# A fused attention, gated MLP and soft mixture-of-experts kernel: the first MLP block is cut in two halves around the second, and its weights are converted in pieces twice as wide

## The chip, the cores and the metric

The kernel runs on one NeuronCore of a Trainium2 chip. The metric is the device time of one execution in microseconds. Five engines work side by side, each through its own queue in order: PE (TensorE, matrix products; PEld loads its stationary operand), DVE (VectorE), ACT (ScalarE), POOL (GpSimd) and SP, which here issues nearly all DMAs.

## The reference, cut to what matters

```python
# 1. linear attention: 4 sequences, 8 heads, 576 positions, head 64, 128 features
def phi(x):
    proj = x @ w_phi
    proj = proj - max(abs(proj), axis=-1)
    return concat([exp(proj), exp(-proj)])
num = phi(q) @ (phi(k).T @ v);  den = phi(q) @ sum(phi(k)) + 1e-6
x = num / den                                  # 2304 tokens x 512
# 2. gated MLP, d_ff 1536
xn = x / sqrt(mean(x * x) + 1e-6) * rms_g
x = (silu(xn @ w_gate) * (xn @ w_val)) @ w_out
# 3. soft mixture of 8 experts, 4 slots each
logits = x @ phi;  d = softmax(logits, over tokens);  c = softmax(logits, over slots)
slot = d.T @ x;  slot_out[e] = relu(slot[e] @ w1[e]) @ w2[e]
return c @ slot_out
```

The MLP weights arrive as 64-bit floats, so the kernel turns them into 32-bit words itself.

## The kernel before, in words

The work falls into three stages. All large products are made of pairs of reduced-precision operands: a value is split into a high part (a cast) and a low part (value minus high part), and three products replace one.

**Key stage.** A loop over 18 tiles of 128 tokens (`TILES`) computes the key features and accumulates keys times values for each of the four sequences. Into its 36 half steps the queries of token block 0 are fitted (class `Turned`; the table `TURNED0` gives the half step of each part), and 16 of the 36 weight pieces are converted.

**MLP stage.** The tokens form 6 blocks of 384 (`BLK`). For each block the loop over `m` runs through 12 slices of 128 of d_ff: `gate` and `val` (12 matmuls each through `wide`, L826) and `out_tile` (9 matmuls, L851 to L853) which adds to three accumulators in PSUM. After each of the three comes a call of `fill()`, so a block has 36 slots; a table says what is done in which slot: the queries of the *next* block (`attend` is the product with keys and values for two heads, `scale` the root mean square, `out` the normalisation) and the softmax part `post` of the block *before* (`PSLOTS`). At the end of a block `split_block` makes the high and low parts of the next one's input `xraw` (ACT cast, DVE subtraction, both recorded as L100 and L103 of the helper `split`).

**Weights.** There are 3 x 6 weight tiles (`g`, `v`, `o` for each pair `j` of slices), each converted in two pieces of 128x512 (class `Conv`): a DMA, an ACT scaling (L125), three integer operations on DVE (L132 to L134), an ACT cast and a POOL subtraction into the weight tile. In block 0 one piece goes into each slot but every fifth, so all are done by slot 25; slice `m` of block 0 needs weight pair `m // 2`.

**Expert stage.** After the last block `finish` does its softmax part: it forms `xo` (the slot inputs), then the combine weights `c3`, turns them (`cturn`, L720) and stores them to memory (`cT_d`); two DMAs issued by ACT bring all combine weights back. Then come `fc1` (L960) and `fc2` (L976) of eight experts and the last product `combine` (L997), whose tiles go out on SP.

The order in each engine's queue is made by a scheduler when the program is built: it starts from the written order, and may put an operation that is ready in its model ahead of one that is not. It is fixed before the run. Buffer counts (`bufs`) limit it.

Of the kernel before, what the change touches and what calls it, by code (L numbers as in the profile page):

```python
# [26 lines left out]
NPRE = 16  # L27
# [3 lines left out]
CSKIP = 5  # L31
PSLOTS = [1, 4, 7, 12, 14, 16, 18, 20, 24]
REDUCED = [0, 0, 2, 3, 5, 6, 4, 8, 7, 11, 12, 9, 14, 12, 17, 18, 15, 20, 18, 23, 24, 27, 30]
TURNED0 = [2, 8, 14, 20, 12, 15, 20, 26, 28, 31]
TURNED1 = [0, 7, 14, 21, 6, 13, 20, 26, 28, 30]
# [26 lines left out]
def tile_kernel(ctx: ExitStack, tc: tile.TileContext, q2T, qT, kT, v, wbd, wg, wv, wo, rmsg, phi, w1, w2, consts, out):  # L62
# [44 lines left out]
    pieces = [(j, nm, c) for j in range(NJ) for nm in "gvo" for c in range(2)]  # L107
# [3 lines left out]
    class Conv:  # L111
# [3 lines left out]
        def __init__(self, sp, wp, key, bufs):  # L115
            self.sp, self.wp, self.key, self.bufs = sp, wp, key, bufs

        def load(self):
            j, nm, c = self.key
            self.raw = self.sp.tile([128, 512, 2], U32, tag="wraw", name="wraw", bufs=self.bufs[0])  # L120
            SP.dma_start(out=self.raw.rearrange("p n w -> p (n w)"), in_=wsrc[nm][j, :, 512 * c:512 * c + 512].bitcast(U32))

        def scale(self):
            self.w = self.wp.tile([128, 512], F32, tag="S", name="wt", bufs=self.bufs[1])
            ACT.activation(out=self.w, in_=self.raw[:, :, 1].bitcast(F32), func=AF.Copy, scale=2.0 ** -112)  # L125

        def join(self):

            w, hi, lo = self.w.bitcast(U32), self.raw[:, :, 1], self.raw[:, :, 0]
            shl, shr, band, bor = ALU.logical_shift_left, ALU.logical_shift_right, ALU.bitwise_and, ALU.bitwise_or  # L130
            return [
                lambda: DVE.tensor_scalar(out=w, in0=w, scalar1=3, scalar2=None, op0=shl),  # L132
                lambda: DVE.scalar_tensor_tensor(out=w, in0=hi, scalar=0x80000000, in1=w, op0=band, op1=bor),
                lambda: DVE.scalar_tensor_tensor(out=w, in0=lo, scalar=29, in1=w, op0=shr, op1=bor),  # L134
            ]

        def parts(self):
            j, nm, c = self.key
            if (nm, j) not in W:
                W[nm, j] = (wpA if j < 3 else wpool["B"]).tile([128, 2, 1024], F32R, tag="w", name=f"w{nm}{j}")  # L140
            u = W[nm, j]
            s = slice(512 * c, 512 * c + 512)
            split(u[:, 0, s], u[:, 1, s], self.w, hi_eng=ACT, lo_eng=POOL)

    conv_at = iter(pieces)
    convs = []

    scaled, joined = [], []

    def conv_load(sp, bufs, *pools):  # L150

        key = next(conv_at, None)
        if key is not None:
            n = pieces.index(key)
            c = Conv(sp, pools[n % len(pools)] if pools else sp, key, bufs)
            c.load()
            convs.append(c)
# [4 lines left out]

    def conv_scale():
        if convs:
            scaled.append(convs.pop(0))
            scaled[-1].scale()

    def conv_join(*between):
        ops = []
        if scaled:  # L170
            joined.append(scaled.pop(0))
            ops = joined[-1].join()
        for n in range(max(len(ops), len(between))):
            for f in between[n] if n < len(between) else ():
                f()
            if n < len(ops):
                ops[n]()
# [15 lines left out]
    class Q:  # L193
# [10 lines left out]
        def attend(self, c):  # L204
            if c == 0:
                xraw[self.blk] = xp.tile([128, 4, BLK], F32, tag="xraw", name="xraw", bufs=1)
# [56 lines left out]
    class Reduced(Q):  # L263
# [43 lines left out]
        def steps(self):  # L307
# [8 lines left out]
            return sorted(zip(REDUCED, s), key=lambda x: x[0])  # L316
# [71 lines left out]
    with ExitStack() as pk:  # L388
# [147 lines left out]
        for _ in range(3):  # L536
            conv_load(sp, (4, 3))
        conv_scale()
# [9 lines left out]
        qsteps = q0.steps(TURNED0[0:4], TURNED0[4:8], TURNED0[8:])  # L548
        qsteps = [[f for m, f in qsteps if m == n] for n in range(2 * TILES)]
        q0.begin()  # L550
        for i in range(TILES):
# [5 lines left out]
            if 0 < i < NPRE - 2:  # L557
                conv_load(sp, (4, 3))
# [11 lines left out]
            if kn:  # L570
                kn.project(0)
                kn.project(1)
                conv_join([lambda: kn.largest(0)], [lambda: kn.less(0), lambda: kn.largest(1)], [lambda: kn.less(1)])
# [61 lines left out]
    with ExitStack() as p2:  # L635
# [10 lines left out]
        def post(blk, x2):  # L646
# [12 lines left out]
            def logits():  # L659
# [7 lines left out]
                Mo, Mn = nM_run[(blk + 1) % 2], nM_run[blk % 2]  # L667
# [3 lines left out]
                DVE.tensor_scalar(out=Mn, in0=mx, scalar1=-1.0, scalar2=Mo if blk else None, op0=ALU.mult, op1=ALU.min if blk else ALU.bypass)  # L671
                if blk:
# [3 lines left out]
                ACT.activation(out=dT, in_=LT, func=AF.Exp, bias=Mn, accum_out=zb if blk else Z_run)  # L676
                if blk:
# [14 lines left out]
            def dispatch():  # L692
# [3 lines left out]
                if blk:  # L696
# [4 lines left out]
            def combine():  # L701
# [241 lines left out]
    with ExitStack() as p3:  # L943
# [60 lines left out]
        for e in range(NE):  # L1004
            fc1(e, 0)
# [79 lines left out]
```

## Time and profile before

| | |
|---|---|
| median of 3 runs | 763.22 us (761.87 to 764.25) |
| profiled execution | 764.22 us, its span 762.4 us |
| TensorE clock granted, mean | 0.98 of full speed |
| busy PE / DVE / ACT / POOL | 95% / 60% / 49% / 21% |
| key stage | 0 to 134.95 us |
| MLP block 0 | 134.95 to 244.95 us |
| MLP block 1 | 244.95 to 338.35 us |
| last accumulation of the MLP ends | 701.6 us |

The span runs from the first to the last instruction; 1.8 us of the time lie around it. The 40-slice view shows PE full from about 220 us to 700 us. Before that and after it there are gaps.

### The profile page before, as it was taken

What the parts mean: (1) busy time and instruction counts of PE and PEld (TensorE: products, weight loads), DVE (VectorE), ACT (ScalarE), POOL (GpSimd) and SP (SyncE); (2) the same over time, 40 slices, a digit from 0 to 9 for tenths busy, and PEclk for the clock granted to TensorE, in tenths of its full rate; (3) what the DMA queues carried; (4) which work ended last, traced back from release to release, by engine and by line L of the source; (5) the groups of instructions that cost most, each with busy time, mean ns of one, the idle gap of its engine ahead of it and who ended that gap; (6) DMA issues with size and microseconds to landing.
All of it is one profiled execution on the core that took longest, in us unless ns stands there. A gap on an engine that the chain in (4) does not pass through costs nothing.

```text
span 762.4 us, 12573 instructions
## 1 busy us (share of the span) xinstructions
PE 722.6 (95%) x4871; PEld 583.3 (77%) x4871; DVE 453.7 (60%) x875; ACT 373.3 (49%) x867; POOL 160.8 (21%) x128
## 2 busy tenths in 40 slices
PE   7997899986899999999999999999999999999895
PEld 4664555974788988899888989889888899988343
DVE  6898777899956556564564555645556453323213
ACT  6889675555744455435564345643465331212102
POOL 2663430446530211012110121101211010000000
PEclk9998999999999999999999999999999999999798
DMA  8762411554301110101000010000100046467698
GB/s 285 249 209 93 140 43 43 173 170 138 111 1 60 42 32 21 47 1 31 23 21 19 1 32 22 21 19 1 32 1 1 9 175 266 171 256 287 263 363 295
DMA packets 27739, 79.47 MB, mean 104 GB/s; under 512 B 2976, under 2 KB 13664, under 8 KB 23584
## 3 DMA queue, kind: packets, MB, share of 16 engines
q1 hardware_dynamic: 27456, 77.79, 29.7%
q10 hardware_dynamic: 224, 0.88, 0.4%
q8 instruction: 38, 0.62, 0.3%
q14 instruction: 21, 0.17, 0.1%
HBM read 71.99 MB, written 6.67 MB: 103 GB/s over the span
## 4 chain that ended last, share of the span: by engine, by line
PE 69%; ACT 1%; DVE 1%; issue 0%; ACTq 0%; DVEq 0%
PE pv L826 18%; PE pg L826 17%; PE acc L851 6%; PE acc L852 6%; PE acc L853 6%; PE num L213 3%; PE y L960 2%; PE y L976 2%; PE den L221 2%; PE x2tp L654 1%; PE qP L283 1%; PE qP L284 1%; PE op L997 1%; PE LT L664 1%; PE sps L695 1%; ACT qe L231 1%
## 5 line engine op out<-in xcount | busy, mean ns | idle before, releaser
L826 PE MATMUL pv<-xnh,wv 128*128 128x384 f32 x576 | 151.3, 343 | 1.0 <-DVE t L838 1.0
L826 PE MATMUL pg<-xnh,wg 128*128 128x384 f32 x576 | 150.0, 342 | 0.9 <-ACT xnh L100 0.5
L826 PEld LDWEIGHTS pg<-xnh,wg 128*128 128x128 f32 x576 | 104.9, 189 | 6.8 <-issue 0.9
L826 PEld LDWEIGHTS pv<-xnh,wv 128*128 128x128 f32 x576 | 102.8, 188 | 8.0 <-issue 6.7
L287 POOL PARTITION_ALL_REDUCE qe<-qe x32 | 50.0, 1563 | 247.1 <-ACT qe L286 227.4
L826 PE MATMUL pg<-xnl,wg 128*128 128x384 f32 x288 | 97.7, 339 | 0.0
L826 PE MATMUL pv<-xnl,wv 128*128 128x384 f32 x288 | 97.7, 339 | 0.0
L851 PE MATMUL acc<-wo,hh 128*128 128x512 f32 x216 | 88.0, 408 | 2.1 <-ACT hh L100 2.1
L852 PE MATMUL acc<-wo,hh 128*128 128x512 f32 x216 | 86.0, 398 | 0.0
L853 PE MATMUL acc<-wo,hl 128*128 128x512 f32 x216 | 85.5, 396 | 0.4 <-POOL hl L103 0.4
L100 ACT CAST hh<-t 128x384 fp32r<-128x384 f32 x72 | 36.7, 510 | 82.6 <-PE acc L852 67.7
L834 DVE SCALAR_TENSOR_TENSOR t<-t,pg 128x384 f32<-128x384 f32 x72 | 39.7, 551 | 52.5 <-ACT t L833 52.4
L833 ACT ACTIVATE t<-pg 128x384 f32<-128x384 f32 x72 | 35.1, 488 | 61.2 <-PE pg L826 61.2
L103 DVE TENSOR_TENSOR hl<-t,hh 128x384 fp32r<-128x384 f32 x62 | 34.5, 557 | 48.3 <-ACT hh L100 46.0
L231 ACT COPY qe<-qe 32x192 f32<-32x192 f32 x128 | 44.8, 350 | 31.7 <-DVE qe L226 30.4
L838 DVE TENSOR_TENSOR t<-t,pv 128x384 f32<-128x384 f32 x72 | 39.7, 551 | 28.9 <-PE pv L826 27.8
L826 PEld LDWEIGHTS pg<-xnl,wg 128*128 128x128 f32 x288 | 54.3, 188 | 0.3 <-DVE xnl L103 0.2
L826 PEld LDWEIGHTS pv<-xnl,wv 128*128 128x128 f32 x288 | 54.1, 188 | 0.1
L465 PE MATMUL kacc<-kp,vt 128*64 128x256 f32 (+1 forms) x320 | 43.5, 400 | 6.2 <-ACT kp L442 6.2
L853 PEld LDWEIGHTS acc<-wo,hl 128*128 128x128 f32 x216 | 40.7, 188 | 10.9 <-POOL hl L103 1.1
L851 PEld LDWEIGHTS acc<-wo,hh 128*128 128x128 f32 x216 | 40.9, 189 | 10.2 <-ACT hh L100 2.8
L852 PEld LDWEIGHTS acc<-wo,hh 128*128 128x128 f32 x216 | 40.8, 189 | 6.4
(202 smaller groups left out, 1241.0 us busy)
## 6 DMA issues: line engine op xcount, KB each, us to landing
eu<-in_w_dram SPq DMA_DIRECT2D x32, 1024.0 KB, 6.3
wraw<-in_wg_dram SPq DMA_DIRECT2D x12, 512.0 KB, 4.2
wraw<-in_wv_dram SPq DMA_DIRECT2D x12, 512.0 KB, 4.2
wraw<-in_wo_dram SPq DMA_DIRECT2D x12, 512.0 KB, 4.3
qraw<-in_qT_dram SPq DMA_DIRECT2D x32, 192.0 KB, 2.3
raw<-in_kT_dram SPq DMA_DIRECT2D x18, 256.0 KB, 4.0
vt<-in_v_dram SPq DMA_DIRECT2D x18, 256.0 KB, 3.9
out_dram<-ob SPq DMA_DIRECT2D x18, 256.0 KB, 3.1
```

What stands on the lines that cost most here:

```text
L100: ACT.copy(out=hi, in_=src)
L103: (lo_eng or POOL).tensor_tensor(out=lo, in0=src, in1=hi.bitcast(F32), op=ALU.subtract)
L231: ACT.copy(out=rd[64 * hh + 32 * r:64 * hh + 32 * r + 32, g], in_=dn[o:o + 32])
L287: POOL.partition_all_reduce(e[:, 0], e[:, 1], channels=128, reduce_op=bass_isa.ReduceOp.absmax)
L465: PE.matmul(out=kva[o0:o0 + 64, hh // 2], lhsT=self.vt[r0:r1, h], rhs=kp[r0:r1, hh].rearrange("p s f -> p (s f)"), start=first and hh < 2, ...
L826: PE.matmul(out=p, lhsT=w[:, a, c], rhs=x, start=n == 0, stop=n == 11)
L833: ACT.activation(out=t, in_=g, func=AF.Tanh, scale=0.5)
L834: DVE.scalar_tensor_tensor(out=t, in0=t, scalar=1.0, in1=g, op0=ALU.add, op1=ALU.mult)
L838: DVE.tensor_tensor(out=t, in0=t, in1=wide("v", m, xs), op=ALU.mult)
L851: PE.matmul(out=acc[i], lhsT=hh[:, s], rhs=w[:, 0], start=m == 0, stop=False)
L852: PE.matmul(out=acc[i], lhsT=hh[:, s], rhs=w[:, 1], start=False, stop=False)
L853: PE.matmul(out=acc[i], lhsT=hl[:, s], rhs=w[:, 0], start=False, stop=m == MF - 1)
```

## The change

- **Order of the MLP.** A list of phases replaces the loop over blocks: block 0 with slices 0 to 5 (18 slots), block 1 with all 12 (36 slots), block 0 with slices 6 to 11 (18 slots), then blocks 2 to 5. At the end of the first phase the three accumulators of block 0 are copied by ACT, halved, into a tile that a DMA writes to memory; it is read back before the third phase ends, and DVE adds it to the second half. `split_block` runs for block 0 twice. Its input `xraw` has a buffer of its own. The `post` of block 1 now comes first (in the third phase, table `PSHORT`), that of block 0 in the fourth.
- **Weights.** 18 pieces of 128x1024 replace 36 of 128x512. Six instead of eight tiles' worth are converted in the key stage, twelve in the MLP, at slots given by `CONVAT` over 40 slots. POOL makes the low part of the hidden values in the first 40 slots (`EARLY`); before, in block 0 until slice 9.
- **Queries.** Block 0's come some half steps earlier (`TURNED0`). The first half of block 1's (head pairs 0 and 1 and the first `attend`) moves into the key stage, the rest must be done by slot 14 instead of 30 (`TURNED1`). Block 2's queries begin at slot 24 of block 1 (`QSHIFT`).
- **Combine weights of the last block.** `cturn` and the two ACT DMAs come after four experts of `fc1` instead of before the first.

```diff
-NPRE = 16
+NPRE = 6
+KCONV, MCONV = 3, 2
-TURNED1 = [0, 7, 14, 21, 6, 13, 20, 26, 28, 30]
+TURNED1 = [-15, -8, 0, 5, -8, 0, 7, 11, 13, 14]
+PHASES = [(0, 0, MF // 2), (1, 0, MF), (0, MF // 2, MF)] + [(b, 0, MF) for b in range(2, NBLK)]
+CONVAT = [0, 3, 7, 12, 16, 19, 22, 25, 28, 31, 34, 37]
+QSHIFT, EARLY = 24, 40
...
-            self.raw = self.sp.tile([128, 512, 2], U32, tag="wraw", name="wraw", bufs=self.bufs[0])
+            self.raw = self.sp.tile([128, 1024, 2], U32, tag="wraw", name="wraw", bufs=self.bufs)
...
+        q1 = Turned(q1p, psk, 1, {"misc": 3, "raw": 1, "pr": 3, "e": 1})
+        q1steps = q1.steps(TURNED1[0:4], TURNED1[4:8], TURNED1[8:], lag=3)
+        q1.begin()
+        qsteps += [(m + 2 * TILES, f) for m, f in q1steps if m < 0]
+        q1steps = [(m, f) for m, f in q1steps if m >= 0]
...
+            if m1 < MF:
+                part = xp.tile([128, TPB, DM], F32, tag=XTAG[1], name="part", bufs=1)
+                for i in range(TPB):
+                    ACT.activation(out=part[:, i], in_=accs[p][i], func=AF.Copy, scale=0.5)
+                SP.dma_start(out=part_d, in_=part)
+                parts[blk] = None
+                return []
+            x2 = [x2_tile() for i in range(TPB)]
+            for i in range(TPB):
+                if blk in parts:
+                    DVE.scalar_tensor_tensor(out=x2[i], in0=accs[p][i], scalar=0.5, in1=parts[blk][:, i], op0=ALU.mult, op1=ALU.add)
+                else:
+                    ACT.activation(out=x2[i], in_=accs[p][i], func=AF.Copy, scale=0.5)
...
+        def fill():
+            n = slot[0]
+            slot[0] += 1
+            for at in CONVAT:
+                if n == at:
+                    conv_scale(piece_words)
+                if at <= n < at + 3:
+                    conv_join()
+                if n == at + 2:
+                    conv_load(sp, MCONV)
+                if n == at + 3:
+                    conv_parts()
+            for f in plan[n]:
+                f()
...
+            if after:
+                hs = split_h(t, slot[0] < EARLY)
...
         for e in range(NE):
+            if e == CTURN:
+                lastturn(ps.tile([96, TPB, 128], F32, tag="op", name="ctp", bufs=5), kl)
+                load_c()
             fc1(e, 0)
```

The queue of DVE at the end of block 1's queries, before. `den`, `e`, `xraw` and `s` belong to the last `attend`, `t` to the MLP, `ms` and `rs` to the root mean square:

```order
L225 TENSOR_SCALAR e_2630<-den 128x192
L226 RECIPROCAL e_2630<-e_2630 128x192
L232 TENSOR_TENSOR xraw<-xraw,e_2630 128x384
L834 SCALAR_TENSOR_TENSOR t<-t,pg 128x384
L239 TENSOR_TENSOR s<-s,e_2630 128x384
L838 TENSOR_TENSOR t<-t,pv 128x384
L250 TENSOR_SCALAR ms<-ssq 128x3
L186 TENSOR_SCALAR rs<-ms 128x3
```

The same place now (`wt` rows are weight conversion):

```order
L221 TENSOR_SCALAR e_2146<-den 128x192
L141 SCALAR_TENSOR_TENSOR wt<-wraw,wt 128x1024
L222 RECIPROCAL e_2146<-e_2146 128x192
L843 SCALAR_TENSOR_TENSOR t<-t,pg 128x384
L143 SCALAR_TENSOR_TENSOR wt<-wraw,wt 128x1024
L847 TENSOR_TENSOR t<-t,pv 128x384
L139 TENSOR_SCALAR wt<-wt 128x1024
L228 TENSOR_TENSOR xraw<-xraw,e_2146 128x384
L141 SCALAR_TENSOR_TENSOR wt<-wraw,wt 128x1024
L235 TENSOR_TENSOR s<-s,e_2146 128x384
L143 SCALAR_TENSOR_TENSOR wt<-wraw,wt 128x1024
L246 TENSOR_SCALAR ms<-ssq 128x3
```

Before, no weight conversion was left when the queue came to the last `attend`; now five conversion operations of two pieces stand between `den` and `ms`, the sixth and seventh of twelve pieces.

The queue of PE around the last product of block 1's normalisation (`r`), before, inside block 0's slice 11:

```order
L826 MATMUL pv<-xnh_1764,wv_2540 128x384 x2
L826 MATMUL pv<-xnl_1765,wv_2540 128x384
L826 MATMUL pv<-xnh_1768,wv_2540 128x384 x2
L365 MATMUL r<-dg,small 128x384
L826 MATMUL pv<-xnl_1769,wv_2540 128x384
L826 MATMUL pv<-xnh_1772,wv_2540 128x384 x2
```

The same product now, at the end of block 0's first half:

```order
L863 MATMUL acc_1861<-wo_2190,hl 128x512
L863 MATMUL acc_1862<-wo_2190,hl 128x512
L244 MATMUL ssq<-small,s 128x1 x3
L861 MATMUL acc_1863<-wo_2190,hh 128x512
L862 MATMUL acc_1863<-wo_2190,hh 128x512
L863 MATMUL acc_1863<-wo_2190,hl 128x512
L361 MATMUL r<-dg,small 128x384
L835 MATMUL pg<-xnh_2321,wg_284 128x384 x2
```

Before, seven matmuls of `val` and nine of `out_tile` stand between `r` and block 1's first `gate`; now three matmuls lie between `ssq` and `r`, and block 1's first `gate` stands right behind `r`.

The queue of PE at the start of the expert stage, before (`stp` gives the slot inputs, `ctp` turns the combine weights, `y` is `fc1`):

```order
L682 MATMUL L<-cst,l 128x96
L791 MATMUL stp<-G,S_run 128x32 x4
L720 MATMUL ctp<-cst,c_7124 96x128 x3
L960 MATMUL y_7145<-eu_6504,xo 32x512 x4
L960 MATMUL y_7145<-eu_6506,xo 32x512 x4
```

And now:

```order
L691 MATMUL L<-cst,l 128x96
L800 MATMUL stp<-G,S_run 128x32 x4
L1015 MATMUL y_6996<-eu_6362,xo 32x512 x4
L1015 MATMUL y_6996<-eu_6364,xo 32x512 x4
L1015 MATMUL y_6996<-eu_6366,xo 32x512 x4
L1015 MATMUL y_6996<-eu_6368,xo 32x512 x4
L729 MATMUL ctp<-cst,c_6982 96x128 x3
```

`ctp` has moved behind four experts of `fc1`.

## Rows read from the trace of the kernel before

**Rows 1.** Busy time of each engine by stretch (us), with granted clock, DMA share:

```profile
60.00:80.00 20.00, 16.04 (x138) 10.65 (x132) 15.81 (x30) 17.44 (x44) 6.17 (x7) 0.83 0.30 99
100.00:120.00 20.00, 19.43 (x186) 11.84 (x180) 14.46 (x25) 15.36 (x36) 7.38 (x8) 1.00 0.19 60
134.40:213.50 79.10, 67.14 (x401) 56.45 (x401) 71.96 (x107) 46.14 (x101) 41.82 (x30) 0.96 0.43 143
```

**Rows 2.** Timeline of PE: first gate of blocks 0, 1 and 2:

```profile
134.95 0.62 PE L826 MATMUL pg<-xnh,wg 128*128 128x384 f32 x2 [0.55 <-ACT xnh L100]
...
244.95 0.52 PE L826 MATMUL pg<-xnh,wg 128*128 128x384 f32 x2
...
338.35 0.52 PE L826 MATMUL pg<-xnh,wg 128*128 128x384 f32 x2
```

**Rows 3.** Waits of PE, 130 to 235 us (total, times, longest):

```profile
PE num L213 <- ACT e L357: 7.8, 4, 2.9
```

**Rows 4.** Timeline of PE: the ends of an out_tile and a projection, starts count:

```profile
144.16 0.39 PE L851 MATMUL acc<-wo,hh 128*128 128x512 f32 x1
...
146.27 0.28 PE L338 MATMUL P<-wbd_h,qxh 128*128 128x256 f32 x1
...
146.62 0.51 PE L826 MATMUL pg<-xnh,wg 128*128 128x384 f32 x2
```

**Rows 5.** The chain that ended last: one gate, one attend (start, us):

```profile
251.54 2.12 PE pg L826 x12
...
284.49 1.44 PE num L213 x8
285.93 0.79 PE den L221 x16
```

**Rows 6.** Groups of DVE by form, 134.4 to 215 us (busy us, mean ns):

```profile
L133 DVE SCALAR_TENSOR_TENSOR wt<-wraw,wt 128x512 uint32<-128x512 uint32 x20 | 22.0, 1098 | 0.4
L134 DVE SCALAR_TENSOR_TENSOR wt<-wraw,wt 128x512 uint32<-128x512 uint32 x20 | 20.7, 1037 | 0.2
L132 DVE TENSOR_SCALAR wt<-wt 128x512 uint32<-128x512 uint32 x20 | 12.0, 601 | 2.5 <-ACT wt L125 2.4
L838 DVE TENSOR_TENSOR t<-t,pv 128x384 f32<-128x384 f32 x8 | 4.3, 538 | 0.0
L226 DVE RECIPROCAL e<-e 128x192 f32<-128x192 f32 x3 | 4.0, 1344 | 0.0
L343 DVE TENSOR_REDUCE qmx<-P 128x2 f32<-128x256 f32 x9 | 3.7, 407 | 0.9 <-PE P L340 0.9
```

**Rows 7.** Timeline of DVE and POOL during weight conversion:

```profile
157.38 0.69 DVE L133 SCALAR_TENSOR_TENSOR wt<-wraw,wt 128x512 uint32<-128x512 uint32 x1
157.47 1.73 POOL L103 TENSOR_TENSOR wv<-wt,wv 128x512 fp32r<-128x512 f32 x1 [1.30 <-ACT wv L100]
158.11 1.64 DVE L134 SCALAR_TENSOR_TENSOR wt<-wraw,wt 128x512 uint32<-128x512 uint32 x1
```

**Rows 8.** Timeline from root mean square to block 1's first high part:

```profile
237.22 0.16 DVE L250 TENSOR_SCALAR ms<-ssq 128x3 f32<-128x3 f32 x1 [0.52 <-PE ssq L248]
...
241.82 0.61 DVE L261 SCALAR_TENSOR_TENSOR xraw<-xraw,small,r 128x384 f32<-128x384 f32 x1 [0.60 <-PE r L365]
...
242.46 1.09 ACT L100 CAST xnh<-xraw 128x384 fp32r<-128x384 f32 x2 [2.06 <-DVE xraw L261]
```

**Rows 9.** PE in the key stage: its longest wait, and that stretch:

```profile
71.78 3.68 PE L465 MATMUL kacc<-kp,vt 128*64 128x256 f32 x16 [3.88 <-ACT kp L442]
...
70.00:80.00 10.00, 8.22 (x56) 4.96 (x58) 7.77 (x15) 7.74 (x21) 2.77 (x3) 0.66 0.29 89
```

**Rows 10.** Expert stage: PE at its start, then stretches as in rows 1:

```profile
712.95 0.87 PE L720 MATMUL ctp<-cst,c 128*96 128x128 f32 x3 [2.09 <-DVE c L715]
...
720.00:745.00 25.00, 25.00 (x318) 11.16 (x310) 3.46 (x6) 1.49 (x6) 1.77 (x1) 1.00 1.01 362
745.00:750.00 5.00, 5.00 (x62) 2.95 (x62) 2.50 (x4) 1.75 (x4) 0.00 (x0) 1.00 0.74 254
```

More of the change, by code (lines that the diff above doesn't have):

```diff
@@ L106, in tile_kernel @@
     W = {}
-    pieces = [(j, nm, c) for j in range(NJ) for nm in "gvo" for c in range(2)]
+    pieces = [(j, nm) for j in range(NJ) for nm in "gvo"]
     wsrc = {"g": wg, "v": wv, "o": wo}
@@ L137, in parts @@
-        def parts(self):
[L138 to L143, printed above, removed]
+            if n == 1:
+                DVE.tensor_scalar(out=w, in0=w, scalar1=3, scalar2=None, op0=ALU.logical_shift_left)
+            elif n == 2:
+                DVE.scalar_tensor_tensor(out=w, in0=hi, scalar=0x80000000, in1=w, op0=ALU.bitwise_and, op1=ALU.bitwise_or)
+            else:
+                DVE.scalar_tensor_tensor(out=w, in0=lo, scalar=29, in1=w, op0=ALU.logical_shift_right, op1=ALU.bitwise_or)
@@ L145, in tile_kernel, with conv_load @@
+        def parts(self):
+            j, nm = self.key
+            u = W[nm, j] = (wpA if j < 3 else wpool["B"]).tile([128, 2, 1024], F32R, tag="w", name=f"w{nm}{j}")
+            split(u[:, 0], u[:, 1], self.w, hi_eng=ACT, lo_eng=POOL)
     conv_at = iter(pieces)
-    convs = []
-    scaled, joined = [], []
-    def conv_load(sp, bufs, *pools):
+    loaded, convs, joined = [], [], []
+    def conv_load(sp, bufs):
         key = next(conv_at, None)
         if key is not None:
-            n = pieces.index(key)
-            c = Conv(sp, pools[n % len(pools)] if pools else sp, key, bufs)
+            c = Conv(sp, key, bufs)
@@ new lines, in tile_kernel, with piece_words @@
+        q1.ps = ps
+        put(0, q1steps)
+        part_d = dp.tile([128, TPB, DM], F32, name="part_d")
+        wtile = wpB.tile([128, 2, 1024], F32, tag="w", name="wt")
+        words = []
+        for _ in range(2):
+            conv_load(sp, MCONV)
+        slot = [0]
+        def piece_words():
+            n = len(words)
+            words.append(n)
+            if n < len(CONVAT) - 1:
+                return wtile[:, n % 2]
+            return xp.tile([128, 1024], F32, tag=XTAG[1], name="wt", bufs=1)
@@ L933, in tile_kernel @@
         for i in range(TPB):
-            out_tile(MF - 1, hs, acc, i)
+            out_tile(p, MF - 1, hs, accs[p], i)
         mctx.close()
@@ L939, in tile_kernel @@
         unit(NX + 19)
-        post(NBLK - 1, [])(acc)
+        lastturn = post(NBLK - 1, [], NBLK - 1)(accs[p])
     with ExitStack() as p3:
```

272 lines of the change are left out of this document (135 added, 137 removed).

## The prediction

> **What bounds the kernel now.** I read the page's table of engines and its 40 slices first, to find where PE is not full; then the busy time by stretch, the timeline of PE at the block borders and its waits; then the queue of DVE where PE waits; last the expert stage.
>
> PE bounds the MLP stage from block 1 on: block 1 lasts 93.4 us, from 244.95 to 338.35 [rows 2], and the slices show PE full there. Block 0 lasts 110.0 us. Its own PE work is less than that. A slice has gate 2.12, val as much, out_tile 2.11 [rows 4, 5], so 6.35, and twelve make 76.2. Block 1's queries add twelve projections of 0.35 [rows 4], 4.2, four attends of 2.23 [rows 5], 8.9, and turns, `ssq` and `r`, some 4.2 by estimate (2.4, 0.9 and 0.9). That is 93.5, so block 0 loses 16.5 us. The waits named for PE there are for the exponentials ahead of `attend`, 7.8 us in four waits [rows 3], but what is late behind them is DVE: it is busy 71.96 of 79.1 us, 91%, while pieces are converted, against 67.14 for PE, at a granted clock of 0.96 [rows 1]. So DVE bounds block 0 for its first 79 us.
>
> The key stage, 135 us, is a mixture: PE is busy 19.43 of 20 us at 100 to 120, but 16.04 at 60 to 80, where it waits 3.88 us for ACT and then runs at a mean clock of 0.66 for ten us [rows 1, 9]. In the expert stage PE waits 2.09 us for the combine weights [rows 10]; from 720 to 745 the DMA engines are full, share 1.01.
>
> **The change part by part.**
>
> *A, key stage.* It takes on half of block 1's queries: six projections (2.1), one attend (2.2), six turns (1.2 by estimate), 5.5 us of PE, with their DVE and ACT work, in half steps 21 to 33, roughly 80 to 125 us. It loses four of its sixteen 512-wide conversions' worth, 2.74 us of DVE each (22.0, 20.7 and 12.0 us for 20 of them, [rows 6]), 10.9 us of DVE. If PE is full, the stage grows by 5.5. If the long wait of rows 9 does not form, because DVE and ACT are less crowded, it loses 3.9 of waiting and about 3.4 of slow clock (0.34 of 10 us): 5.5 less 7.3, about -2; with the small gaps of 80 to 100 also filled, -5. The bounds are -5 and +5.5. I take 0: PE fills its gaps of 60 to 100, the wait is partly there.
>
> *B, MLP up to the point where PE is full again.* The work of PE behind the key stage falls by the same 5.5. What counts is the time lost. The order of DVE shows that seven pieces stand ahead of `ms`, and that PE has nothing left at block 1's border but three matmuls between `ssq` and `r`. So block 1 cannot begin before DVE has gone through that queue. One 1024-wide piece: twice 2.74 less three fixed parts of about 0.1 (0.69 for 512 columns against 0.54 for 384 [rows 6, 7], so some 0.61 go with the columns), 5.2. Without a busy POOL beside it: two operations of 2 x 0.69 and one of about 0.9, 3.6. POOL is busy 41.82 of 79.1 us before [rows 1]; now it has in this stretch seven low parts of twice 1.4 and six of the hidden values at 1.2, 27 of some 65 us. So I take 4.7, nearer the row with POOL in it.
>
> The queue until `dg`: seven pieces 32.9; six slices of two operations at 0.54, 6.5; six projections of two operations at 0.41, 4.9; three attends of 0.36, 1.34 and two of 0.55, 8.4; the root mean square, eleven operations of 0.16 [rows 8] and one of 0.56, 2.3. Sum 55.0. In front lie 3.2 (gate, tanh and hand-over), behind it two more conversion operations, 2.8, while `r` runs, and 1.2 from the first normalisation to the first high part [rows 8]: 62.2 with DVE never idle, 67.6 with the 91% of rows 1. PE's own work there is 6 x 6.35, three attends, six projections, turns and `ssq`, `r`: 49.8. So 12.4 to 17.8 are lost, I take 15. After the border DVE has 4.3 pieces (20.2), splits and normalisation (4.6) and the slices' operations (4.4), 29.2, or 32 at 91%, while PE has 25.4 of matmuls to the fifth gate: 4 more, bounds 0 and 7. The loss is 19 against 16.5: with the 5.5 that moved, -3.0. With 3.6 a piece and no idle time it is 5 (then -17), with 5.2 and 91% it is 29 (then +7).
>
> [...] In rows 7 a DVE operation that takes 0.69 by itself takes 1.64, and ends 0.55 after the POOL operation does that began before it (159.20 and 159.75). [...]
>
> *C, what is added.* Three ACT copies of 128x512 lie beside gate and val; the write and the read of 786 KB have more than a block between them; block 0's second split is of an input long ready. POOL's low parts of hidden values now queue behind weight parts of 2.8 us instead of 1.4; out_tile has 4.2 us of gate and val ahead of it, so 0.5 + 2.8 + 1.2 is just too late at times. Post and queries of blocks 1 and 2 in 18 slots: PE has some 49 us there, DVE some 38. I take +0.5, bounds 0 and +3.
>
> *D, expert stage.* The wait of 2.09 us for the combine weights goes, and PE starts on `fc1` that much earlier; `ctp` itself stays. SP's queue now holds the write of the combine weights, which waits for four experts, in front of eight weight loads. ACT's read waits for that write, with its copy of `fc1`'s result behind it; both come about when they did. Past 745 us the stores decide: the DMA engines are full before and at 0.74 for 5 us [rows 10], so at most 1.3 us can be taken up there. I take -1.3, bounds -2.5 and +1.
>
> Sum: 0 - 3.0 + 0.5 - 1.3 = -3.8, from the profiled execution's 764.2 us (span 762.4 and 1.8 around it) 760.4. That execution is 1.0 above the median of the three runs, whose spread is 2.4; I say 760.0.
>
> **Rivals.**
>
> *R1, the queue of DVE decides (slower).* Place: the end of block 0's first half. Pieces cost 5.2 or more because POOL holds its operations of 2.8 us, so DVE reaches `ms` later, and the third attend's exponentials, behind ACT casts that themselves wait for DVE, come some 7 us late. The loss is 27 to 29, B +5 to +7; A and C at 0 and +1, D -1.3: 768 to 771. It decides from about 23 us lost in B. For it: the hoisted conversion in the order, 91% busy, rows 7. Against: the total of DVE's work in the MLP stage hardly grows, and block 1 has no post.
>
> *R2, both stalls go (much faster).* Conversion costs near 4 us a piece, the loss in B is about 12, so B is -10; A is -1. With C and D 752 to 753. For it: fewer, larger operations, and block 1's slices spread the rest. Against: the order has not spread the pieces over 40 slots as the table says, but put seven ahead of `ms`.
>
> *R3, nothing to measure.* The key stage is bound by PE where the queries go (19.43 of 20), A is +4, and takes back what B gives: 763 to 764.
>
> [...]
>
> **How the numbers follow.** The forecast has 0.40, own range 757 to 763; R1 0.25, R2 0.17, R3 0.18. What a measurement can tell from no change is about 0.3%, 2.3 us: faster is below 760.9, slower above 765.5. Of the forecast's share 0.28 lie below 760.9, of R2's all: faster 0.45. R1 gives slower 0.25 and R3's upper end 0.02, so 0.27; the rest, 0.28, is no change. The range runs from 752 (R2) to 769 (into R1); about 0.2 lie outside.
>
> **What would show it.** In the changed profile: A is right if the first gate starts at 133 to 137 us, and there is no wait of PE near 4 us at 60 to 80. B is right if block 1's first gate comes 62 to 68 us after block 0's, with DVE above 85% busy between them, and PE waits there for `ssq`, `r` and the first high part; L141 and L143 should take 1.7 to 1.9 us in the mean. C is right if the groups of acc show no waits above 1 us on POOL. D is right if `fc1` begins some 2.4 us after `stp` begins and stores end one us or so sooner relative to it. The forecast is wrong if block 1's gate comes later than 70 us (R1), earlier than 58 (R2), or the first gate after 139 (R3).

## The result and the profile after

The changed kernel takes 775.12 us (median of 769.06, 773.13, 777.10 and 782.47) against 762.84 before; the medians differ by 1.6%. The ratio, 1.0126 with a 95% interval of 1.0094 to 1.0158, leaves out the last of these times, since it lies over 1.5% above the fastest. The forecast was 760.0 and the range 752 to 769, so it was wrong in sign and in range. Two things have to be explained: the profiled execution, 769.06 us, is 4.8 longer than the one before, and the other executions of the same program are 4 to 13 longer still, where the kernel before repeats within 2.4.

In what follows, the border is the place where block 0's first half ends and block 1's first gate starts, and "gate to gate" is the time from block 0's first gate to that one. A held operation is one that is recorded as busy for longer than it takes by itself. All stretches are read from single profiled executions.

The timeline of PE after the change, in answer to [rows 2, 9, 10]: the key stage's wait, the first gates of blocks 0, 1 and 2, the last `out_tile`, and the start of `stp` and `fc1`.

```profile
73.75 2.00 PE L461 MATMUL kacc<-kp,vt 128*64 128x256 f32 x16 [1.44 <-DVE mx L420]
...
136.91 0.61 PE L835 MATMUL pg<-xnh,wg 128*128 128x384 f32 x2 [0.20 <-ACT xnh L107]
...
205.62 1.01 PE L835 MATMUL pg<-xnh,wg 128*128 128x384 f32 x2 [1.25 <-ACT xnh L107]
...
345.74 0.62 PE L835 MATMUL pg<-xnh,wg 128*128 128x384 f32 x2 [0.37 <-ACT xnh L107]
...
710.39 0.39 PE L863 MATMUL acc<-wo,hl 128*128 128x512 f32 x1
...
718.13 1.08 PE L800 MATMUL stp<-G,S_run 96*128 96x32 f32 x8 [0.19 <-DVE S_run L797]
719.64 0.64 PE L1015 MATMUL y<-eu,xo 128*32 128x512 f32 x4 [0.43 <-DVE xo L801]
```

The first gate and the last `out_tile` cut the profiled execution in three. The first gate is 2.0 us later than before (136.91 for 134.95). From it to the last `out_tile` it is 573.5 us for 566.3, 7.2 more (before, that instruction starts at 701.2). From there to the end of the span it is 56.9 for 61.2, 4.3 less. The sum is 4.9, the difference of the spans (767.3 and 762.4).

The busy time by stretch, columns as in [rows 1]; the third number from the end is the granted clock:

```profile
60.00:80.00 20.00, 18.38 (x180) 10.95 (x177) 16.21 (x26) 18.89 (x46) 8.81 (x9) 1.00 0.27 75
...
136.90:205.60 68.70, 55.50 (x330) 45.83 (x330) 58.34 (x79) 38.93 (x76) 27.67 (x14) 0.90 0.41 147
181.47:184.88 3.41, 3.41 (x28) 1.86 (x25) 1.17 (x3) 2.96 (x5) 1.46 (x2) 0.50 0.00 0
195.12:205.60 10.48, 5.40 (x13) 3.27 (x13) 8.72 (x19) 3.75 (x5) 2.67 (x2) 0.50 0.44 156
205.60:245.60 40.00, 36.00 (x169) 32.35 (x170) 30.16 (x31) 16.92 (x26) 21.42 (x10) 0.92 0.31 109
...
700.00:720.00 20.00, 17.96 (x111) 13.46 (x113) 8.74 (x30) 5.30 (x16) 0.95 (x1) 1.00 0.84 314
```

The waits of PE from block 0's first gate to block 1's (total, times, longest):

```profile
PE num L209 <- ACT e L353: 4.5, 1, 4.5
PE r L361 <- DVE dg L249: 3.5, 1, 3.5
PE acc L863 <- POOL hl L110: 2.5, 1, 2.5
PE pg L835 <- ACT xnh L107: 1.4, 2, 1.3
```

With 1.5 of smaller ones PE waits 13.4 us there; by the row of the whole stretch it is idle 13.2 of 68.7. The mean clock of 0.90 counts idle time as well. It comes from the two shorter rows: 13.9 us at a granted clock of 0.50. PE is busy in 8.8 of them and, by an estimate from the 0.50, loses half of that, 4.4 us. Without these 4.4 its 55.5 busy us are 51.1, and in a later run (e7) it is busy 51.12 over the same stretch at a clock of 1.00. So the 68.7 us are 51.1 of work, 13.2 of waiting and 4.4 of slow clock. Behind the border, to 346 us, PE is idle another 5.8 us, 3.8 of it `acc` waiting for `hl` and most of the rest for the splits of the blocks' inputs. Two more stretches at 0.50, with 6.6 us of work in them, add 3.3 by the same estimate.

Why DVE is late at the border is seen where its operations stand against POOL's. Groups of DVE by form from 137 to 240 us, in answer to [rows 6]:

```profile
L143 DVE SCALAR_TENSOR_TENSOR wt<-wraw,wt 128x1024 uint32<-128x1024 uint32 x12 | 22.0, 1830 | 0.1
L141 DVE SCALAR_TENSOR_TENSOR wt<-wraw,wt 128x1024 uint32<-128x1024 uint32 x12 | 18.3, 1525 | 0.2
L139 DVE TENSOR_SCALAR wt<-wt 128x1024 uint32<-128x1024 uint32 x12 | 10.5, 875 | 3.9 <-ACT wt L132 3.8
L235 DVE TENSOR_TENSOR s<-s,e 128x384 f32<-128x384 f32 x3 | 6.1, 2049 | 0.2 <-ACT e L234 0.2
...
L182 DVE TENSOR_SCALAR rs<-ms 128x3 uint32<-128x3 uint32 x1 | 2.0, 2050 | 0.0
```

A piece takes 4.23 us (the first three rows), less than the 4.7 of the prediction. But the sum of squares `s`, 0.555 us in the mean in the kernel before, takes 2.05 in the mean, and an operation on three columns 2.05, which took 0.17 before. The timeline of DVE and POOL shows what runs beside them:

```profile
176.12 3.17 POOL L110 TENSOR_TENSOR wg<-wt,wg 128x1024 fp32r<-128x1024 f32 x1 [3.59 <-ACT wg L107]
...
177.00 2.70 DVE L235 TENSOR_TENSOR s<-s,e 128x384 f32<-128x384 f32 x1
...
191.35 2.79 POOL L110 TENSOR_TENSOR wo<-wt,wo 128x1024 fp32r<-128x1024 f32 x1 [8.38 <-ACT wo L107]
...
192.14 2.42 DVE L235 TENSOR_TENSOR s<-s,e 128x384 f32<-128x384 f32 x1 [0.22 <-ACT e L234]
...
194.11 1.30 POOL L110 TENSOR_TENSOR hl<-t,hh 128x384 fp32r<-128x384 f32 x1
...
195.47 1.22 PE L863 MATMUL acc<-wo,hl 128*128 128x512 f32 x2 [2.53 <-POOL hl L110]
...
197.65 2.37 POOL L110 TENSOR_TENSOR wg<-wt,wg 128x1024 fp32r<-128x1024 f32 x1 [2.24 <-ACT wg L107]
...
198.00 2.05 DVE L182 TENSOR_SCALAR rs<-ms 128x3 uint32<-128x3 uint32 x1
```

Each of the three DVE operations begins while a low part runs on POOL and ends within 0.5 us of that part's end (179.70 and 179.29; 194.56 and 194.14; 200.05 and 200.02). The first and the third stand on the path: the exponentials for the next `num` write the buffer that the first `s` still reads, and `dg` follows the third operation. The second does not decide by itself. `ssq` needs it, but `ssq` stands on PE behind matmuls that wait until 195.47 for `hl`, and POOL begins `hl` only when the same low part is done. The two rows of `s`, which has two inputs, take 2.70 and 2.42 us for 0.555, and the third operation, with a single input, 2.05 for 0.17. By what means POOL holds them, no row shows.

### The profile page after: what moved, and what is told of

It reads as the page before. It is cut to its first block, busy times and chain, and to the rows that moved or that the text cites. A ratio compares the mean times of both kernels' runs of the same rounds, so it can differ in the third digit from the quotient of the medians.

```text
span 767.3 us, 12412 instructions
## 1 busy us (share of the span) xinstructions
PE 725.2 (95%) x4871; PEld 585.4 (76%) x4871; DVE 451.8 (59%) x824; ACT 369.4 (48%) x835; POOL 165.6 (22%) x114
## 4 chain that ended last, share of the span: by engine, by line
PE 73%; DVE 7%; DMA 7%; ACT 6%; issue 3%; POOL 3%; SPq 0%; POOLq 0%; ACTq 0%; DVEq 0%
PE pv L835 17%; PE pg L835 16%; PE acc L861 6%; PE acc L862 6%; PE acc L863 6%; PE num L209 4%; PE kacc L461 4%; DMA eu<-in_w_dram 3%; PE den L217 2%; PE kacc L470 2%; ACT e L227 2%; DVE wt L143 1%; DMA qraw<-in_q2T_dram 1%; DVE s L235 1%; DMA cT<-cT_d 1%
## 5 line engine op out<-in xcount | busy, mean ns | idle before, releaser
L110 DVE TENSOR_TENSOR hl<-t,hh 128x384 fp32r<-128x384 f32 x58 | 32.3, 557 | 45.9 <-ACT hh L107 45.9
L863 PEld LDWEIGHTS acc<-wo,hl 128*128 128x128 f32 x216 | 41.1, 191 | 17.8 <-POOL hl L110 8.0
```

Of the source, the lines that this page charges most:

```text
L110: (lo_eng or POOL).tensor_tensor(out=lo, in0=src, in1=hi.bitcast(F32), op=ALU.subtract)
L863: PE.matmul(out=acc[i], lhsT=hl[:, s], rhs=w[:, 0], start=False, stop=m == m1 - 1)
```

## Experiments

Each is an edit of the changed kernel, or of the kernel before where it says so; ratios are to runs of the kernel before on the same chip. Two theories recur. By Q, the length of DVE's queue ahead of the border decides. By L, POOL's low parts do, since they hold single operations of DVE and keep the hidden values waiting on POOL.

**e1, two pieces later.** The table's later slots are moved, and the later loads are made to wait for a value of block 1.

```
-CONVAT = [0, 3, 7, 12, 16, 19, 22, 25, 28, 31, 34, 37]
+CONVAT = [0, 3, 7, 18, 21, 24, 27, 30, 33, 36, 39, 42]
...
+            if after is not None:
+                ACT.copy(out=self.raw[:, 0].bitcast(F32), in_=after[:, 0:2])
...
-                    conv_load(sp, MCONV)
+                    conv_load(sp, MCONV, t if n >= 18 else None)
```

> Five pieces instead of seven are converted ahead of block 1's border: the loads of the later ones wait for a value of block 1 (by a copy of 128x2 on ACT into the tile that the load then fills). Theory Q (the length of DVE's queue ahead of the border decides): two pieces of 4.2 us leave the queue, block 1's first gate comes 60 to 62 us after block 0's (68.7 in the changed kernel), and the kernel is 5 to 8 us faster than the changed one. Theory L (single DVE operations are held while POOL has a low part of 2.7 us, and hidden values stand behind the low parts on POOL): the small operations at the border are still held by the pieces that stay, 66 to 69 us, and the time moves by less than 2 us.

Measured: 779.44 (768.31 to 783.90), ratio 1.0107 (1.0036 to 1.0177). Block 1's gate comes 61.6 us after block 0's (143.33 and 204.95), as theory Q had it, but nothing is gained. From the border to the last `out_tile` it is 8.6 us longer than in the changed kernel; the largest new wait there is one of 5.4 us at 293 us, for the exponentials of block 2's queries, which POOL prepares from 290 us on, behind the low part of a piece. The other loss is at the first gate, at 143.33 for 136.91, in a key stage that this edit does not touch. The same stretch of it in this kernel, and in the profile of the changed one:

```profile
104.00:118.00 14.00, 14.00 (x63) 6.64 (x64) 5.82 (x15) 4.47 (x11) 1.45 (x2) 0.51 0.07 19
```

```profile
104.00:118.00 14.00, 14.00 (x128) 8.46 (x127) 9.39 (x21) 8.41 (x20) 2.93 (x4) 1.00 0.14 40
```

PE is busy all the time in both, and gets through 63 instructions where it got through 128: the clock stands at 0.51 in the mean for 1.00. What it did before the fall, in e1:

```profile
101.13 0.36 PE L415 MATMUL P<-wbd_h,xh 128*128 128x256 f32 x1 [0.61 <-DVE pr L426]
...
101.68 0.73 PE L246 MATMUL ssq<-small,s 128*128 128x1 f32 x6
102.34 1.08 PE L463 MATMUL kacc<-kp,vt 64*64 64x256 f32 x8
103.35 0.64 PE L472 MATMUL kacc<-kp,small 64*32 64x256 f32 x8
```

A wait of 0.61 us, six matmuls of one column, and then those of the tile in which two sequences meet, with 64 rows instead of 128 (the half-height tile). The changed kernel's profiled execution has the same instructions and the same wait of 0.61 there, and no fall. In the kernel before, `ssq` stands at 118, amid whole projections.

**e2, low parts halved.**

```
-            split(u[:, 0], u[:, 1], self.w, hi_eng=ACT, lo_eng=POOL)
+            ACT.copy(out=u[:, 0], in_=self.w)
+            for s in (slice(0, 512), slice(512, 1024)):
+                POOL.tensor_tensor(out=u[:, 1, s], in0=self.w[:, s], in1=u[:, 0, s].bitcast(F32), op=ALU.subtract)
```

> The low part of a piece is made by two POOL operations of 128x512 instead of one of 128x1024; nothing else. Theory L: no DVE operation between 137 and 230 us is held by more than 1.5 us (now s 2.70 and 2.42 for 0.55, rs 2.05 for 0.16, wt 3.30 for 1.22), no wait of PE for hl is over 1.3 us (now 2.53 and 2.07), gate to gate 64 to 66 us, 3 to 5 us faster than the changed kernel. Theory Q: DVE has the same work in the same order, 68 to 70 us, within 1.5 us of the changed kernel.

Measured: 778.78 (772.05 to 780.86), ratio 1.0170 (1.0110 to 1.0229), gate to gate 66.1 us (145.21 to 211.30), with the fall in the key stage again (0.59 from 104 to 118, and the first gate 8.3 us later than in the changed kernel's profile). The timeline of DVE and POOL behind `ssq`:

```profile
203.40 2.51 POOL L150 TENSOR_TENSOR wg<-wt,wg 128x512 fp32r<-128x512 f32 x2
...
203.78 0.16 DVE L248 TENSOR_SCALAR ms<-ssq 128x3 f32<-128x3 f32 x1 [1.53 <-PE ssq L246]
203.97 0.73 DVE L184 TENSOR_SCALAR rs<-ms 128x3 uint32<-128x3 uint32 x1
...
204.74 1.19 DVE L185 TENSOR_SCALAR rs<-rs 128x3 uint32<-128x3 uint32 x1
```

At this place halving does not help: the hold is shorter, but the next small operation is held by the second half, 1.92 us for the two, where one took 2.05. Elsewhere it does. `s` takes 1.31 us in the mean for 2.05, the longest wait for `hl` is 1.9 us for 2.5 (1.3 was expected), and gate to gate is 2.6 us less, close to the 64 to 66 of theory L and below the 68 to 70 of theory Q. From the first gate to the last `out_tile` it is 571.0 us for 573.5. The 2.5 us do not show in the time, since the key stage loses more. So the remedy works in part, and a shorter hold is still a hold.

**e3, the late turns alone, on the kernel before.**

```
...
-                combine()
-                cturn()
+                combine(kl)
+                return cturn
...
         for e in range(NE):
+            if e == CTURN:
+                lastturn(ps.tile([96, TPB, 128], F32, tag="op", name="ctp", bufs=5), kl)
+                load_c()
             fc1(e, 0)
```

> The kernel before with one part of the change alone: the last block's combine weights are turned, written and read after four experts of fc1. If the gain of 4.3 us that the changed kernel shows behind the last block comes from this part (a wait of 2.1 us and the ten us at half clock that follow it), it is 3 to 5 us faster than before, and the granted clock stays at 1.00 from 700 to 740. If, as the prediction had it, the stores at the end take up all but 1.3 us, it is 0.5 to 2 us faster, and the slow clock is seen again or gone without a gain.

Measured: 759.72 (759.02 to 760.57), ratio 0.9939 (0.9918 to 0.9961): 4.1 us faster. The clock over 700 to 720 us is 1.00; before, it was 0.74. There it stood at 0.50 from 708.55 to 718.79, from 2.3 us ahead of the wait for the combine weights on, and PE was busy 8.0 of these 10.2 us, so by estimate half of that, 4.0, was lost. First the kernel before, then e3:

```profile
700.00:720.00 20.00, 16.79 (x103) 8.53 (x106) 8.03 (x31) 3.79 (x13) 0.98 (x2) 0.74 0.69 267
```

```profile
700.00:720.00 20.00, 18.37 (x153) 8.48 (x155) 8.73 (x32) 4.45 (x15) 2.76 (x2) 1.00 0.83 299
```

**e4, low parts on DVE.**

```
-            split(u[:, 0], u[:, 1], self.w, hi_eng=ACT, lo_eng=POOL)
+            split(u[:, 0], u[:, 1], self.w, hi_eng=ACT, lo_eng=POOL if j < 2 else DVE)
```

> The low parts of the twelve pieces in the MLP stage are made by DVE instead of POOL, which keeps the hidden values' alone. Theory L: DVE does 1.2 us more a piece, but its other operations are no longer held (4.2 us a piece now, of which 3.1 is what they take by themselves), so a piece with its low part takes 4.3 to 4.5; hidden values wait for nothing, gate to gate 62 to 66 us, 3 to 7 us faster than the changed kernel. Theory Q: seven pieces put 8 us more into the queue ahead of the border, 72 to 77 us, 4 to 8 us slower.

Measured: 768.12 (765.12 to 773.15), ratio 1.0061 (1.0035 to 1.0087). A piece with its low part takes 4.66 us on DVE, and without it, held by POOL, it took 4.23: POOL's hold had cost nearly as much as the work that POOL took over. The same three `s` as in the changed kernel now take:

```profile
L235 DVE TENSOR_TENSOR s<-s,e 128x384 f32<-128x384 f32 x3 | 2.1, 712 | 0.3 <-ACT e L234 0.3
```

That is 0.71 us in the mean for 2.05, and the operation on three columns takes 0.97 for 2.05. The waits for POOL behind the border are gone. At the border the queue is left: PE waits 2.95 for `s` and 5.95 for `dg`, since two pieces' operations now stand between `ms` and `dg`.

**e5, `ssq` moved in the key stage.**

```
-TURNED0 = [2, 7, 12, 17, 12, 14, 18, 23, 25, 27]
+TURNED0 = [2, 7, 12, 17, 12, 14, 18, 23, 29, 31]
```

> The changed kernel with block 0's scale and out issued later in the key stage (steps 29 and 31 instead of 25 and 27): on PE, ssq and r move behind block 0's last attend, away from the tile where two batches meet, whose matmuls have 64 rows. In two profiles of the variants so far, with the same key stage as the changed kernel, the granted clock stood at 0.50 from 104 to 118 us, in the profile of the changed kernel and in another it did not. Theory C (the short wait and the one-column matmuls of ssq just ahead of the half-height tile let the clock fall there in some executions, 6 to 7 us each time): no fall at 100 to 120, first gate at 136 to 138, the runs lie within 4 us of each other, median 767 to 771. Rival (the half-height tile does it by itself, or the fall comes anywhere): a fall in the key stage again, first gate at 139 to 146, runs spread over 8 us or more, median 773 to 779.

Measured: 771.75 (770.95 to 772.44), ratio 1.0102 (1.0077 to 1.0127), just above the 767 to 771 expected. The runs, 13 us apart in the changed kernel, lie within 1.5. The stretch that had half clock in e1:

```profile
104.00:118.00 14.00, 13.90 (x134) 8.46 (x136) 7.25 (x13) 10.69 (x26) 2.88 (x4) 1.00 0.14 34
```

The first gate is at 139.70, outside the 136 to 138 expected: the clock stood at 0.50 for 3.4 us each from 21 and from 76 us in this execution.

**e6 and e7, low parts on DVE and two pieces held back, and the same with `ssq` moved.** The edits of e4 and e1, with the table as it was and the condition below; e7 adds that of e5.

```
+                    conv_load(sp, MCONV, t if 14 <= n <= 18 else None)
```

> Low parts of the MLP stage's pieces on DVE as in the run before, and the loads of the sixth and seventh piece wait for a value of the fifth slice of block 0 and the first of block 1 (an ACT copy of 128x2 into the tile), so that five pieces stand ahead of block 1's ssq instead of seven, and none between ms and dg where two stood. If the queue of DVE at the border is what is left (waits of 2.95 for s and 5.95 for dg, then 16 us at half clock), block 1's first gate comes 56 to 61 us after block 0's (65.9), and it is 5 to 8 us faster than with the low parts alone, where no clock falls in the key stage 760 to 763. If the waits only move into block 1, as in the first run of later pieces, it is within 3 us of it.

> The same with ssq moved in the key stage as well. If both reasons hold and add up, the runs lie close together at 758 to 763, level with or below the kernel before; if the key stage's clock falls are not tied to ssq, 763 to 771 with a spread of 6 us or more.

Measured: e6 760.63 (753.90 to 765.24), ratio 0.9942 (0.9910 to 0.9973); e7 753.93 (751.79 to 756.54), ratio 0.9860 (0.9829 to 0.9891). e6's runs spread over 11 us, e7's over 5. e7 is below the 758 to 763 expected. In e6's profile, the slowest of its ten executions, the key stage has its fall (0.59 from 104 to 118, first gate 146.08), in e7's it has not. The border in e7, and the stretch ahead of it:

```profile
138.62 0.62 PE L837 MATMUL pg<-xnh,wg 128*128 128x384 f32 x2 [0.20 <-ACT xnh L107]
...
187.97 0.80 PE L246 MATMUL ssq<-small,s 128*128 128x1 f32 x6 [1.78 <-DVE s L237]
...
191.88 0.88 PE L363 MATMUL r<-dg,small 128*128 128x384 f32 x2 [0.90 <-DVE dg L251]
...
194.02 0.62 PE L837 MATMUL pg<-xnh,wg 128*128 128x384 f32 x2 [1.25 <-ACT xnh L107]
```

```profile
138.60:194.00 55.40, 51.12 (x330) 43.71 (x330) 46.49 (x76) 34.36 (x72) 9.39 (x7) 1.00 0.36 125
```

Gate to gate is 55.4 us for 68.7, at a granted clock of 1.00.

**e8, the kernel before with late turns and low parts on DVE.** Added to e3's edit:

```
-            split(u[:, 0, s], u[:, 1, s], self.w, hi_eng=ACT, lo_eng=POOL)
+            split(u[:, 0, s], u[:, 1, s], self.w, hi_eng=ACT, lo_eng=POOL if pieces.index(self.key) < NPRE else DVE)
```

> The kernel before with the late turns and with the low parts of the MLP stage's 20 pieces of 128x512 on DVE. If POOL's low parts hold DVE there as well (the three operations of a piece take 2.74 us in the mean, by themselves about 1.7, with the low part 2.4), DVE has some 6 us less to do in block 0, block 0 takes 103 to 107 us instead of 110 and the kernel 753 to 757 us. If the holds cost nothing there because each of POOL's operations is short, DVE has more to do and block 0 takes 110 to 114 us, the kernel 759 to 763.

Measured: 750.72 (750.29 to 753.40), ratio 0.9835 (0.9806 to 0.9863), 9.0 below e3 and below the 753 to 757 expected. The stretch of the last row of [rows 1]:

```profile
134.40:213.50 79.10, 75.32 (x467) 66.96 (x468) 74.60 (x131) 50.78 (x114) 13.94 (x12) 0.98 0.43 142
```

PE is busy 75.32 us for 67.14. DVE is no less busy, 74.60 for 71.96: its three operations and the low part take 2.87 us a piece, where the three alone took 2.74.

**e9 and e10, each of e7's two edits alone, on e5.**

```
-            split(u[:, 0], u[:, 1], self.w, hi_eng=ACT, lo_eng=POOL)
+            split(u[:, 0], u[:, 1], self.w, hi_eng=ACT, lo_eng=POOL if j < 2 else DVE)
```

```
+            if after is not None:
+                ACT.copy(out=self.raw[:, 0].bitcast(F32), in_=after[:, 0:2])
...
-                    conv_load(sp, MCONV)
+                    conv_load(sp, MCONV, t if 14 <= n <= 18 else None)
```

> The kernel with ssq moved (771.75 us, runs within 1.5 us), and the low parts of the MLP stage's pieces on DVE: one of the two edits of the 753.9 us kernel alone. Two pieces still stand between ms and dg. If POOL's low parts cost mainly behind the border (hidden values queued behind them, DVE held), 5 to 7 us go, 764 to 767, gate to gate 65 to 67 (69.4), no wait for POOL. If DVE's queue is all there is to it, more DVE work gains nothing: 770 to 776.

> The kernel with ssq moved, and only the loads of the sixth and seventh piece made to wait, low parts on POOL: the other edit alone. If the queue ahead of the border is a cause by itself, gate to gate 58 to 62 us, 762 to 766. If the holds by POOL keep the border late or the pieces left out come back as waits in block 1, 766 to 771; with the edits adding up, the sum of both gains is 17 to 18 us.

Measured: e9 761.82 (759.44 to 765.31), ratio 0.9978 (0.9956 to 1.0000), gate to gate 65.8 us; e10 768.34 (764.62 to 770.60), ratio 1.0052 (1.0032 to 1.0072), 61.8 us. From 771.75 the low parts alone gain 9.9, the pieces held back alone 3.4, both together 17.8, which is 4.5 more than the sum. Ahead of the border the queue is the larger part: gate to gate falls from 69.4 us by 3.6 in e9, by 7.6 in e10 and by 14.0 with both (e7). But with low parts on POOL the pieces held back return behind the border as waits for hidden values: 5.9 of the 6.2 us in the first row stand there, while the wait in the second row is ahead of it (e10, from 138 to 300 us):

```profile
PE acc L865 <- POOL hl L110: 6.2, 5, 2.6
PE num L211 <- ACT e L355: 4.5, 1, 4.5
```

**e11, hidden values' low parts on DVE, on e5.**

```
-QSHIFT, EARLY = 24, 40
+QSHIFT, EARLY = 24, 0
```

> The kernel with ssq moved, and the low parts of the hidden values of the MLP stage on DVE from the first slices on, those of the pieces on POOL: it tells the queue on POOL (hidden values behind low parts of 2.7 us) from the hold of DVE. If the queue on POOL is what the move of the low parts gains, the waits for hl (6.3 us) and the slow clock behind them go, 765 to 768. If the hold of DVE is, DVE gets 0.56 us more a slice and is held as before, gate to gate 70 to 74 us, 771 to 777.

Measured: 774.60 (774.02 to 776.26), ratio 1.0141 (1.0125 to 1.0157), gate to gate 75.3 us. The waits for POOL go (6.3 us), and the kernel is 2.9 slower: what leaves POOL's queue goes to a DVE that has more to do, and PE waits 5.5 us for `dg`, 3.5 in e5. So e11 shows that this is no remedy, but not what the queue on POOL costs by itself; e9 takes away both the hold and the queue and gains 9.9.

**e12, fewer pieces in the key stage, on e8.**

```
-NPRE = 16
+NPRE = 12
```

> The kernel before with late turns and low parts on DVE (750.7 us), with 12 instead of 16 pieces of 128x512 converted in the key stage, as many columns as in the changed kernel. If the key stage's wait of 3.9 us and the half clock behind it come from the conversion work there, the wait falls under 2 us and the first gate comes at 129 to 132 instead of 134.2; the MLP stage takes four pieces of 2.9 us more on a DVE that is 96% busy, 8 to 12 us for PE less what its own work covers. Sum: 750 to 756 if DVE decides, 745 to 748 if the wait was the dearer.

Measured: 747.79 (747.61 to 749.81), ratio 0.9793 (0.9777 to 0.9809), the fastest kernel here. In the timeline of PE, its longest wait between 60 and 80 us and the first gate, and then that stretch as in [rows 1]:

```profile
68.81 0.36 PE L418 MATMUL P<-wbd_h,xh 128*128 128x256 f32 x1 [1.39 <-ACT kp L442]
...
128.35 0.62 PE L827 MATMUL pg<-xnh,wg 128*128 128x384 f32 x2 [0.55 <-ACT xnh L101]
```

```profile
60.00:80.00 20.00, 18.43 (x177) 12.14 (x178) 17.68 (x34) 19.28 (x49) 7.33 (x10) 1.00 0.21 65
```

The wait and the half clock of [rows 9] are gone, and the first gate comes 5.9 us earlier than in e8 (134.24). The time falls by 2.9 us. In the profiled executions the stretch from the first gate to the last `out_tile` gives back 4.7 (560.9 us for 556.2), and the expert stage is 2.2 shorter.

## Why the prediction was wrong

Of the 15.1 us between the forecast and the median, 8.7 show in the profiled execution (A 2.0, B and C 9.7, D -3.0, counted from 760.4). The rest is the spread between executions, of which the clock in the key stage explains a part.

**A, the key stage (0, bounds -5 and +5.5).** In the profiled execution it was +2.0, and the wait of [rows 9] fell to 1.44 us, as said. Fewer pieces are worth 5.9 (e12; 7.3 was written, with 3.4 for a slow clock that counted idle time too: PE is busy 5.3 of the 6.8 us at 0.50 there, which is 2.7). The queries, 5.5 by estimate, cost up to the 8.6 between the first gates of e12 and the changed kernel (128.35 and 136.91), whose key stages differ in the width of the pieces as well. What the step left out is the clock. With `ssq` ahead of the half-height tile it fell for some 14 us in three of five profiles with that key stage (e1, e2 and e6; first gate 143.33, 145.21 and 146.08), beyond the bounds of A, and in none of five with `ssq` elsewhere (e5, e7, e9, e10, e11). A part of the changed kernel's spread goes with it: e5's four runs lie within 1.5 us, though e9's and e10's, with the same key stage, lie within 6. Which of the longer executions of the changed kernel had the fall is not shown, since they have no trace. By an estimate from 14 us at 0.51 (e1) in some 770, one fall takes 0.009 off the mean clock; 777.10 us (0.973 for the profiled 0.983) fits one, 773.13 (0.980) has too little for one and 782.47 (0.966) more.

**B, the first half of block 0, and with it C: the step that failed.** From the first gate to the last `out_tile` the prediction had -2.5 us (B -3.0, C +0.5), and the profiles show +7.2, a miss of 9.7. Ahead of the border it is 3.9: the forecast took 64.8 us, 49.8 of PE's work and 15 lost, and it was 68.7, past its upper end of 67.6. The step that failed is the price of POOL's low parts. The prediction charged them to DVE's pieces alone, at 4.7 each; it took the small operations of the path at what they take by themselves, and gave the hidden values behind the low parts 0.5 us. In the runs a piece takes 4.23, while `s` three times and the first operation of the root mean square take 8.2 us where 1.8 stood in the sum, and PE waits for hidden values 2.5 us ahead of the border and 3.8 behind it. With the low parts off POOL (e9 against e5) gate to gate is 3.6 us shorter and the rest to the last `out_tile` 5.3, together 8.9 (gates of e5 at 139.70 and 209.09, of e9 at 137.18 and 202.95; last `out_tile` 713.95 and 702.51). That is near the miss but not the same quantity, since e9 also gives DVE the low parts' own work. How the 8.9 divide between the hold of DVE and the queue on POOL is open.

What the sum lacked is not what the change made worse, for the kernel before pays for POOL's low parts too. Off POOL, its stretch from the first gate to the last `out_tile` falls by 10.0 us (e3 to e8, 566.2 to 556.2), that of the changed order by 8.9 (e5 to e9, 574.3 to 565.3). With them off POOL in both, the changed order is still 9.1 longer, and with two pieces held back it is level (e7, 556.0). The work there is not quite the same: the changed order converts four 512-wide pieces' worth more in this stretch and has 5.5 us of queries less. Against e12, which converts as much there (560.9), e9 is 4.4 longer and e7 4.9 shorter. With the low parts on POOL, holding the two pieces back takes off 5.2 of the 8.0 by which e5 exceeds the kernel before (e10, 569.0). So what the change itself costs is the queue of DVE ahead of the border. That mechanism the prediction had: seven pieces did stand ahead of `ms`, and two of them are worth 7.6 us there (e10).

The terms ahead of the border compare as follows. DVE's work came out as summed, 58.3 busy us against 57.8, but by errors that cancel: conversion took 29.9 for 35.7, the held operations 6.4 more than written. DVE was idle 15% of the stretch, where the upper end allowed 9%. PE's own work was 51.1 for 49.8. The slow clock, 4.4 us ahead of the border, stood in no term, although [rows 9] had shown such a stretch.

**B and C behind the border (4 and 0.5).** The other 5.8 us of the miss lie here, 4.0 up to block 2's gate and 1.8 in blocks 2 to 5; e9 takes nothing off the 1.8, and their cause is open. The prediction had the hidden values on POOL "just too late at times", which is the right mechanism with too small a size, and no wait above 1 us as the sign that C is right. PE waited for them 6.3 us in all, up to 2.07 at a time behind the border, and the clock stood at 0.50 for 3.4 us after the longest wait.

**D (-1.3, bounds -2.5 and +1).** It was -4.3, and e3 gives 4.1 by itself. The direction held, the size was wrong twice. The slow clock around the wait (4.0 us) was not priced, and the full DMA engines of [rows 10] do not bound the end as argued: with an earlier start their share from 700 to 720 rises from 0.69 to 0.83, and the stores begin 6 us sooner behind the last `out_tile`. That the late turns keep the clock up is not shown, though: e6, e7 and e9 have them too, and the first 32 matmuls of `fc1` took 6.21, 6.55 and 6.18 us there, where those of e5 took 3.64.

**The rivals.** R1 named 768 to 771, a loss over 23 us in B and POOL's holds. The profiled execution shows 769.1, with 17.6 us of waits and slow clock ahead of the border and 9.1 behind it. Its place and its cause were right, its price of 5.2 a piece was not: the pieces were cheaper, the small operations on the path were dear. Its time is in part luck: A was 2 above and D 3 below what R1 took, and the median of 775.12 lies above its range. R1 had 0.25 and should have had more.

With all three repairs the changed order still gains nothing over the old one: e7 has a ratio of 0.9860 (0.9829 to 0.9891), and e8, the old order with late turns and low parts on DVE, 0.9835 (0.9806 to 0.9863); e12, with fewer pieces in the key stage, has 0.9793.

Not shown: whether the fall comes from the short wait, the one-column matmuls, the half-height tile or something else; e5 moved `ssq`, and none of the five profiles with that edit has the fall.

## What to carry to other kernels

A wait of PE is priced with the clock around it: look in the windows for stretches at 0.50, and add, by estimate, half of PE's busy time in them, not of their whole length (before, 4.0 for 8.0 busy of 10.2 us, beside a wait of 2.09; e3, with neither, is 4.1 us faster). Before moving work to an idle engine, look at the durations of the smallest operations of its neighbour; three columns that took 2.05 us for 0.17 were a hold here, and a total that stays the same can still hide a hold on the path. A loss found in the new kernel is the price of the change only if the old one does not pay it as well: make the same repair in both (e8 beside e9). When executions of one program spread, compare the clock of the same instructions in two traces before looking for a cause in the order.

## What the runs showed of the hardware

The granted clock went to 0.51 in the mean of 14 us with PE busy for all 14.00 of them and a wait of 0.61 us shortly in front, at 101.13 (e1), and was 1.00 over the same 14 us in the changed kernel's profile, where the same instructions and a wait of 0.61 us, at 100.96, stand in front. For an operation with one input of three columns DVE took 2.05 us beside a low part on POOL, and 0.17 in the kernel before. Giving the low parts to a DVE that was 91% busy (71.96 of 79.1 us in the kernel before) made the kernel 9.0 us faster (759.72 in e3, 750.72 in e8).
